# The sign and exponent biases of a top-k attention kernel, made by VectorE in place of ScalarE

## The chip, the cores and the metric

The kernel runs on one core of one Trainium2 chip, as one launch. The metric is the device time of that launch in microseconds, the median of three runs. TensorE (PE), VectorE (DVE), ScalarE (ACT), GpSimd (POOL) and SyncE (SP) work through their own lists in program order, so the order in which the program writes the instructions down is the schedule.

## The reference, cut to what matters

```python
scores = scale * np.matmul(q, k.transpose(0, 1, 3, 2))      # (4, 8, 576, 576), scale = 1/8
kth = np.partition(scores, -32, axis=-1)[..., -32:-31]       # the 32nd largest of each row
scores = np.where(scores >= kth, scores, -1e9)
attn = np.exp(scores - max) ; attn = attn / (sum + 1e-9)     # max, sum over the row
x = (attn @ v), heads side by side: (2304, 512)
h = np.maximum(np.maximum(x @ w1, x @ w2), x @ w3)           # a dense layer, 768 wide
x = h @ w_out
...                                                          # then 8 experts, top 1, 1024 wide
```

## The kernel before, in words

The attention is cut into 144 tiles of 128 query rows by 576 keys, and four tiles make a group `g`, one tile of it having the number `i`. A hand-written loop over a step number `t` issues, at each step, one stage of each of some twelve tiles: the scores of tile t + 2 (PE, L892), the copy of the scores of tile t + 1 out of PSUM into `s` (ACT, L899), the candidate maxima of tile t (DVE, six L921 of 96 columns each, into `c`), and so on back to the product with v of tile t - 14. The dense layer and the first expert slots are fitted in between as units, and from about 700 us on the rest of the experts runs alone (the tail).

The top 32 of a row are found so. On DVE `st_rounds` takes the 48 candidates of a tile through three rounds of eight: L936 writes the eight largest to `T1`, L937 strikes them out, L938 and L939 do the same once more, and L940 writes the third eight to `T3`. The 24th largest candidate (`T3[..., 7]`), with its sign turned and a hair smaller, is the bias `bf`: on ACT, `st_over` takes `Sign(s + bf)` into `g` and counts (L967). On POOL L973 takes `s - g`, and DVE's L982 takes eight maxima of that. From the count and these eight, DVE picks the 32nd value of four tiles at once (L988 to L991, then L1011 and L1012 into `hkth`). L991 also compares with `bf`. Two tiles of a group are then masked on DVE (L1056, `e<-s,hkth,e`), two by way of a second Sign on ACT (L1042) and a subtraction on POOL (L1045). ACT takes the exponential (L1051) with the bias `be`, which is the row's largest value (`T1[..., 0]`) times a constant, for four tiles at once. ACT and POOL then split the result into two float16 halves (L1062, L1066).

What sets the order around the change: `st_rounds` of tile t - 1 is a *chain*, a list of small steps. After each instruction of the `bulk` list (the L921 pairs, the L982, the masks and the subtractions of the splits) `micro` issues one step of each open chain, and `finish` issues what is left of this chain at the end of the step. `st_thr` and `st_over` of tile t - 2 are called straight from the loop, so on ACT `bf` (L957), in every fourth tile also `be` (L946), and the Sign stand behind the L899 of the same step. Where `general` is true, the code belongs to a second attempt, which runs only if the first one missed; it did not run here.

```python
nc.scalar.activation(out=be[g], in_=T1[g][:, :, 0:1], func=ACTF.Copy, scale=-ESC)                          # L946, 128x4
nc.scalar.activation(out=bf[g][:, i], in_=T3[g][:, i, 7:8], func=ACTF.Copy, scale=-(1.0 - 2.0 ** -21))     # L957, 128x1
nc.scalar.activation(out=gg[n], in_=Ss[n], func=ACTF.Sign, bias=bf[g][:, i], accum_out=cnt[g][:, i])       # L967
```

`T1`, `T3`, `bf`, `be`, `cnt`, `s` and `e` lie in SBUF. The tile `vec`, with `y8`, lies in PSUM.

Of the kernel before, what the change touches and what calls it, by code (L numbers as in the profile page):

```python
# [7 lines left out]
F32 = mybir.dt.float32  # L8
# [3 lines left out]
ACTF = mybir.ActivationFunctionType  # L12
ALU = mybir.AluOpType
# [6 lines left out]
def kernel(  # L20
# [14 lines left out]
    nc = tc.nc  # L35
# [5 lines left out]
    P = 128  # L41
# [23 lines left out]
    ESC = 1.0 / (float(D) ** 0.5 * SC * SC * DOWN)  # L65
# [16 lines left out]
    G = 4  # L82
# [12 lines left out]
    def attempt(ctx, general):  # L95
# [531 lines left out]
        with ExitStack() as p1:  # L627
# [3 lines left out]
            sm_p = p1.enter_context(tc.tile_pool(name="sm", bufs=3))  # L631
# [47 lines left out]
            def chain(fns):  # L679
                chains.append(list(fns))  # L680
                return chains[-1]
# [198 lines left out]
            Sps, Ss, T1, T3, zz, bf, be, cnt, y8, kth, ff, ee, pt = ({} for _ in range(13))  # L880
# [43 lines left out]
            def st_rounds(n):  # L924
                g, i = divmod(n, G)
                if i == 0:
                    T1[g] = sm_p.tile([P, G, 8], F32, tag="T1", name="T1", bufs=2)
                    if not general:
                        T3[g] = sm_p.tile([P, G, 8], F32, tag="T3", name="T3", bufs=2)
                if general:  # L930
                    return chain([lambda: nc.vector.max(out=T1[g][:, i], in_=Ss[n])])
                c = cands.pop(n)
                c2 = sm_p.tile([P, CAND * 8], F32, tag="c2", name="c2", bufs=1)
                t2 = sm_p.tile([P, 8], F32, tag="t2", name="t2", bufs=1)
                ops = [
                    lambda: nc.vector.max(out=T1[g][:, i], in_=c),  # L936
                    lambda: nc.vector.match_replace(out=c2, in_to_replace=T1[g][:, i], in_values=c, imm_value=LOW),  # L937
                    lambda: nc.vector.max(out=t2, in_=c2),  # L938
                    lambda: nc.vector.match_replace(out=c, in_to_replace=t2, in_values=c2, imm_value=LOW),  # L939
                    lambda: nc.vector.max(out=T3[g][:, i], in_=c),  # L940
                ]
                return chain(ops)

            def st_bias(g):
                be[g] = sm_p.tile([P, G, 1], F32, tag="be", name="be")
                nc.scalar.activation(out=be[g], in_=T1[g][:, :, 0:1], func=ACTF.Copy, scale=-ESC)  # L946

            def st_thr(n):
                g, i = divmod(n, G)
                if general:  # L950
                    if i == G - 1:
                        st_bias(g)
                    return
                if i == 0:
                    cnt[g] = sm_p.tile([P, G, 1], F32, tag="cnt", name="cnt")
                    bf[g] = sm_p.tile([P, G, 1], F32, tag="bf", name="bf")
                nc.scalar.activation(out=bf[g][:, i], in_=T3[g][:, i, 7:8], func=ACTF.Copy, scale=-(1.0 - 2.0 ** -21))  # L957
                if i == G - 1:
                    st_bias(g)

            def st_over(n):

# [595 lines left out]
            with tc.manual_schedule():  # L1558
# [42 lines left out]
                while second is None or not fin() or len(ranked) < NTT:  # L1601
# [12 lines left out]
                    if ok(t - 1):  # L1614
                        must.append(st_rounds(t - 1))
# [27 lines left out]
                    if ok(n):  # L1643
                        st_thr(n)
                        st_over(n)
# [127 lines left out]
```

## Time and profile before

| | |
|---|---|
| median of 3 runs | 924.04 us (923.32 to 924.06) |
| the profiled execution | 919.08 us, of which 917.4 us lie between its first and last instruction (the span) |
| busy over the span | PE 741.1 us (81%), DVE 745.3 (81%), ACT 705.7 (77%), POOL 597.5 (65%) |
| L957 on ACT | 144 times, from 28.1 to 662.4 us |
| L946 on ACT | 36 times, from 47.0 to 662.4 us |

Busy time is the time in which an engine has at least one instruction of the program in work, waits inside an instruction among it. Neighbouring instructions of DVE and of ACT overlap by some 0.1 us, so what an instruction costs its engine is the distance from its start to the next one's start, and not its duration. In a list of waits the engine on the left was idle, and the instruction on the right of the arrow is what ended it. The chain is the work that ended last, followed back from the last instruction.

### The profile page before, as it was taken

The page shows a single profiled execution, that of the slowest core. Times are in us where ns is not written, and L with a number is a line of the kernel's source. Part 1 is how long each engine was busy: PE and PEld are TensorE (multiplying, and loading weights), DVE is VectorE, ACT ScalarE, POOL GpSimd, SP SyncE. Part 2 cuts the span into 40 slices and gives each one's busy share as a digit, 9 for nine tenths or more (in the row PEclk, how much of TensorE's full clock was granted, in tenths as well). Part 3 has the DMA queues.
Part 4 walks back from the last instruction along what each step waited for, and adds up shares of the span by engine and source line. Part 5 has one row for each costly group of instructions (what it writes and reads, how often), then busy time and mean ns, then how long its engine had stood idle before and what let it go on. Part 6 is the DMA issues. An engine that isn't in the chain of part 4 may idle for free.

```text
span 917.4 us, 29131 instructions
## 1 busy us (share of the span) xinstructions
PE 741.1 (81%) x10606; PEld 573.4 (63%) x10606; DVE 745.3 (81%) x3108; ACT 705.7 (77%) x1464; POOL 597.5 (65%) x554
## 2 busy tenths in 40 slices
PE   1112367888878799978988899989999999999993
PEld 0000236576655678757767688757987756687882
DVE  5999998999999999999998999998852426476661
ACT  4768999999999999999997999998862231566661
POOL 2556788898988699887877889888992220211110
PEclk9999999999998999999989999999999999999997
DMA  9872977767997888799989788988977459699270
GB/s 223 262 232 51 222 148 152 128 135 133 194 167 162 157 153 169 150 201 173 175 167 172 167 158 155 179 173 148 188 153 128 128 170 298 173 298 258 60 223 16
DMA packets 372164, 155.93 MB, mean 170 GB/s; under 512 B 331931, under 2 KB 348319, under 8 KB 372000
## 3 DMA queue, kind: packets, MB, share of 16 engines
q1 hardware_dynamic: 368128, 143.10, 75.0%
q0 software_dynamic: 3136, 9.46, 3.3%
q8 instruction: 87, 1.43, 0.7%
q10 hardware_dynamic: 736, 1.32, 0.4%
q14 instruction: 77, 0.63, 0.2%
HBM read 76.06 MB, written 16.67 MB: 101 GB/s over the span
## 4 chain that ended last, share of the span: by engine, by line
PE 29%; ACT 20%; issue 19%; DVE 17%; POOL 8%; DMA 4%; SPq 1%; POOLq 0%; ACTq 0%; DVEq 0%
PE mm L355 15%; ACT g L967 4%; DVE c L921 4%; PE av L1085 4%; ACT s L899 3%; PE S L892 3%; ACT e L1051 3%; ACT phl L1062 2%; POOL phl L1066 2%; DVE vec L982 2%; POOL f L973 2%; PE mm L1178 2%; DVE e L1056 2%; PE mm L1179 2%; PE mm L1180 2%
## 5 line engine op out<-in xcount | busy, mean ns | idle before, releaser
L355 PEld LDWEIGHTS <-W 128*128 128x128 f16 x4560 | 248.5, 100 | 19.6 <-issue 16.5
L355 PE MATMUL mm<-xT,W 128*128 128x128 f16 x3456 | 214.3, 224 | 13.3 <-DVE vl L746 5.6
L973 POOL TENSOR_TENSOR f<-s,g 128x576 f32<-128x576 f32 x144 | 184.1, 1278 | 40.4 <-ACT g L967 24.2
L1066 POOL TENSOR_TENSOR phl<-e,phl 128x576 f16<-128x576 f32 x144 | 188.2, 1307 | 6.5 <-ACT phl L1062 5.7
L921 DVE MAX8 c<-s 128x8 f32<-128x96 f32 x864 | 175.0, 243 | 9.4 <-ACT s L899 5.6
L892 PEld LDWEIGHTS <-qT 128*128 128x128 f16 (+1 forms) x640 | 56.6, 107 | 189.8 <-issue 155.2
L892 PE MATMUL S<-kt,qT 128*128 128x64 f16 (+3 forms) x320 | 61.9, 345 | 107.2 <-ACT s L899 91.5
L1051 ACT ACTIVATE e<-s,be 128x576 f32<-128x576 f32 x144 | 109.8, 762 | 14.6 <-POOL phl L1066 10.9
L1085 PE MATMUL av<-vh,pt 128*128 128x65 f16 (+3 forms) x1600 | 110.6, 200 | 11.4 <-DVE xn L1134 9.8
L967 ACT ACTIVATE g<-s,bf 128x576 uint16<-128x576 f32 x144 | 111.7, 775 | 5.6
L982 DVE MAX8 vec<-f 128x8 f32<-128x576 f32 x144 | 108.7, 755 | 4.7 <-POOL f L973 1.9
L1045 POOL TENSOR_TENSOR s<-s,g 128x576 f32<-128x576 f32 x72 | 92.6, 1286 | 24.0 <-DVE e L1056 22.3
L1085 PEld LDWEIGHTS <-pt 128*128 128x128 f16 (+3 forms) x2400 | 89.3, 103 | 24.2 <-issue 11.0
L899 ACT ACTIVATE s<-S 128x576 f32<-128x576 f32 x144 | 91.6, 636 | 12.3 <-PE S L892 11.9
L1062 ACT ACTIVATE phl<-e 128x576 f16<-128x576 f32 x144 | 96.2, 668 | 5.9 <-DMA pt<-phl 5.9
L1085 PE MATMUL av<-vl,pt 128*128 128x64 f16 (+3 forms) x800 | 100.1, 197 | 0.0
L461 DVE SCALAR_TENSOR_TENSOR W<-st,W 128x1024 f16<-128x1024 f32 x56 | 65.8, 1220 | 37.3 <-ACT W L460 28.7
L1056 DVE SCALAR_TENSOR_TENSOR e<-s,hkth,e 128x576 f32<-128x576 f32 x72 | 85.4, 1186 | 12.7 <-ACT e L1051 8.0
L892 PE MATMUL S<-kT,qT 128*128 128x512 f16 (+3 forms) x320 | 48.6, 292 | 22.5 <-ACT s L899 22.4
L1169 POOL TENSOR_TENSOR hhl<-a,hhl 128x384 f16<-128x384 f32 x36 | 37.6, 1046 | 33.5 <-ACT hhl L1168 32.3
L460 ACT ACTIVATE W<-st 128x1024 f16<-128x1024 f32 x56 | 55.6, 1046 | 1.8 <-DMA st<-in_moe_w_dram 1.8
L1042 ACT ACTIVATE g<-s,hkth 128x576 uint16<-128x576 f32 x72 | 54.7, 760 | 0.0
(233 smaller groups left out, 1568.6 us busy)
## 6 DMA issues: line engine op xcount, KB each, us to landing
st<-in_moe_w_dram SPq DMA_DIRECT2D x72, 512.0 KB
st<-in_moe_w_dram SPq DMA_DIRECT2D x28, 256.0 KB
raw<-in_moe_w_dram SPq DMA_DIRECT2D x12, 512.0 KB
st<-in_v_dram SPq DMA_DIRECT2D x16, 256.0 KB
hs<-he SPq DMA_DIRECT2D x16, 256.0 KB
hTe<-hs SPq DMA_DIRECT2D x8, 512.0 KB
st<-in_q_dram SPq DMA_DIRECT2D x15, 256.0 KB
qT<-qT SPq DMA_DIRECT2D x30, 128.0 KB
```

The lines of the kernel that those rows point to most:

```text
L355: nc.tensor.matmul(out=ps[:, o * n:(o + 1) * n], lhsT=w(b, kk, c), rhs=x(a, kk), start=(kk == 0 and i == 0), stop=(kk == KD - 1 and i == 2))
L892: nc.tensor.matmul(out=ps[o:o + m, j, 0:(REM if j else NQ * P)], lhsT=qt[:, vv, hh, 0:m], rhs=kr[:, hh] if j else km[:, hh // HG, :, hh % HG],
L899: nc.scalar.activation(out=s, in_=Sps.pop(n).rearrange("p a b -> p (a b)")[:, 0:S], func=ACTF.Copy, scale=DOWN)
L921: nc.vector.max(out=c[:, i * 8:(i + 1) * 8], in_=s[:, i * CW:(i + 1) * CW])
L967: nc.scalar.activation(out=gg[n], in_=Ss[n], func=ACTF.Sign, bias=bf[g][:, i], accum_out=cnt[g][:, i])
L973: let_in(nc.gpsimd.tensor_tensor(out=ff[n], in0=Ss[n], in1=gg.pop(n).bitcast(F16), op=ALU.subtract))
L982: bulk.append(lambda: nc.vector.max(out=y8[g][:, i, 1:9], in_=y))
L1051: nc.scalar.activation(out=e, in_=Ss.pop(n) if early(n) else Ss[n], func=ACTF.Exp, scale=ESC, bias=be[g][:, i])
L1056: masked.append(nc.vector.scalar_tensor_tensor(out=e, in0=Ss.pop(n), scalar=kth[g][:, i:i + 1], in1=e, op0=ALU.is_ge, op1=ALU.mult))
L1062: nc.scalar.activation(out=ph[:, 0, 0:S], in_=p, func=ACTF.Copy)
L1066: nc.gpsimd.tensor_tensor(out=ph[:, 1, 0:S], in0=p, in1=ph[:, 0, 0:S], op=ALU.subtract)
L1085: nc.tensor.matmul(out=av[o:o + m, i, 0:n], lhsT=t[0:kk, p * NCH + c, o:o + m], rhs=v_rows(x, b, c, hh)[:, 0:n], start=(c == 0 and p == 0 ...
```

## The change

DVE makes both biases. `bf` becomes the last step of the chain of `st_rounds`, and in the fourth tile of a group `be` becomes the step before it; in the other tiles that step is empty, so that an instruction of `bulk` can come between L940 and `bf`. `st_thr` no longer does anything in the attempt that runs. From L957 on, line numbers of the changed kernel are lower by one.

```diff
                     lambda: nc.vector.max(out=T3[g][:, i], in_=c),
                 ]
+                if i == 0:
+                    cnt[g] = sm_p.tile([P, G, 1], F32, tag="cnt", name="cnt")
+                    bf[g] = sm_p.tile([P, G, 1], F32, tag="bf", name="bf")
+                ops.append((lambda: st_bias(g)) if i == G - 1 else None)
+                ops.append(lambda: nc.vector.tensor_scalar(out=bf[g][:, i], in0=T3[g][:, i, 7:8], scalar1=-(1.0 - 2.0 ** -21),
+                                                           scalar2=None, op0=ALU.mult))
                 return chain(ops)
 
             def st_bias(g):
                 be[g] = sm_p.tile([P, G, 1], F32, tag="be", name="be")
-                nc.scalar.activation(out=be[g], in_=T1[g][:, :, 0:1], func=ACTF.Copy, scale=-ESC)
+                nc.vector.tensor_scalar(out=be[g], in0=T1[g][:, :, 0:1], scalar1=-ESC, scalar2=None, op0=ALU.mult)
...
-                if i == 0:
-                    cnt[g] = sm_p.tile([P, G, 1], F32, tag="cnt", name="cnt")
-                    bf[g] = sm_p.tile([P, G, 1], F32, tag="bf", name="bf")
-                nc.scalar.activation(out=bf[g][:, i], in_=T3[g][:, i, 7:8], func=ACTF.Copy, scale=-(1.0 - 2.0 ** -21))
-                if i == G - 1:
-                    st_bias(g)
```

ACT's order, at the last two tiles of the tenth group, some 203 to 209 us into the span: before,

```order
L899 ACTIVATE s<-S 128x576
L957 ACTIVATE bf<-T_2707 128x1
L967 ACTIVATE g,cnt<-s,bf 128x576
L1051 ACTIVATE e<-s,be 128x576
L1062 ACTIVATE phl_148<-e 128x576
L1051 ACTIVATE e<-s,be 128x576
L1168 ACTIVATE hhl<-a 128x384
L899 ACTIVATE s<-S 128x576
L957 ACTIVATE bf<-T_2707 128x1
L946 ACTIVATE be<-T_2706 128x4
L967 ACTIVATE g,cnt<-s,bf 128x576
L1042 ACTIVATE g<-s,hkth 128x576
```

and with the change:

```order
L899 ACTIVATE s<-S 128x576
L966 ACTIVATE g,cnt<-s,bf 128x576
L1050 ACTIVATE e<-s,be 128x576
L1061 ACTIVATE phl_148<-e 128x576
L1050 ACTIVATE e<-s,be 128x576
L1167 ACTIVATE hhl<-a 128x384
L899 ACTIVATE s<-S 128x576
L966 ACTIVATE g,cnt<-s,bf 128x576
L1041 ACTIVATE g<-s,hkth 128x576
```

The Sign follows the copy of the scores directly, and the two small instructions are gone; nothing else has moved on ACT.

DVE's order, at the end of the step that makes the thresholds of the last of these tiles (at 204 us): before,

```order
L939 MATCH_REPLACE c<-t_3029,c_3028 128x48
L1163 TENSOR_TENSOR a<-a,mm 128x384
L940 MAX T_2707<-c 128x8
L921 MAX c<-s 128x8 x2
L936 MAX T_3091<-c 128x8
L1219 TENSOR_SCALAR se<-se 128x1
```

and with the change:

```order
L939 MATCH_REPLACE c<-t_3030,c_3029 128x48
L1162 TENSOR_TENSOR a<-a,mm 128x384
L940 MAX T_2710<-c 128x8
L952 TENSOR_SCALAR be<-T_2709 128x4
L946 TENSOR_SCALAR bf<-T_2710 128x1
L921 MAX c<-s 128x8 x2
L936 MAX T_3094<-c 128x8
L1218 TENSOR_SCALAR se<-se 128x1
```

Both biases stand between L940 and the first L921 of the next tile.

DVE's order one step earlier (at 200 us), where the bulk list still holds something when L940 is issued: before,

```order
L988 TENSOR_TENSOR hsel<-vec,cnt 128x36
L940 MAX T_2707<-c 128x8
L746 TENSOR_TENSOR hl<-mm,hl 128x8x64
L1163 TENSOR_TENSOR a<-a,mm 128x384
L990 COPY vec<-T_2342 128x4
L991 SCALAR_TENSOR_TENSOR heq<-vec,bf 128x4
```

and with the change:

```order
L987 TENSOR_TENSOR hsel<-vec,cnt 128x36
L940 MAX T_2710<-c 128x8
L746 TENSOR_TENSOR hl<-mm,hl 128x8x64
L1162 TENSOR_TENSOR a<-a,mm 128x384
L946 TENSOR_SCALAR bf<-T_2710 128x1
L989 COPY vec<-T_2345 128x4
L990 SCALAR_TENSOR_TENSOR heq<-vec,bf 128x4
```

`bf` comes two instructions behind L940 here. Of the 144, 40 stand as at the place above, directly behind L940 or with only `be` between; 10 stand between L990 and L991, 6 between two of L863, L866 and L868, and 88 elsewhere.

## Rows read from the trace of the kernel before

**Rows 1.** The page, part 1: busy us, share of the span, instructions.

```profile
PE 741.1 (81%) x10606; PEld 573.4 (63%) x10606; DVE 745.3 (81%) x3108; ACT 705.7 (77%) x1464; POOL 597.5 (65%) x554
```

**Rows 2.** Stretches: from:to, length, each engine's busy us (x), clock, DMA share, GB/s.

```profile
30.00:100.00 70.00, 15.29 (x78) 7.23 (x78) 68.10 (x241) 54.27 (x118) 41.75 (x37) 1.00 0.66 177
100.00:600.00 500.00, 423.88 (x6370) 338.57 (x6370) 474.94 (x2263) 467.25 (x1029) 430.68 (x372) 0.97 0.85 163
500.00:600.00 100.00, 93.68 (x1566) 78.06 (x1563) 96.35 (x449) 94.63 (x211) 86.09 (x75) 0.98 0.84 166
600.00:665.00 65.00, 61.65 (x906) 49.05 (x904) 56.11 (x270) 57.97 (x130) 57.94 (x51) 0.97 0.93 168
```

**Rows 3.** DVE's waits from 100 to 600 us: us in total, times, longest.

```profile
DVE e L1056 <- ACT e L1051: 5.0, 10, 1.1
DVE hl L746 <- ACT mm L745: 5.0, 5, 2.7
DVE c L921 <- ACT s L899: 2.2, 5, 0.9
DVE W1h L746 <- ACT mm L745: 1.1, 2, 0.8
```

**Rows 4.** The page, part 4: the chain that ended last, by engine.

```profile
PE 29%; ACT 20%; issue 19%; DVE 17%; POOL 8%; DMA 4%; SPq 1%; POOLq 0%; ACTq 0%; DVEq 0%
```

**Rows 5.** ACT's L957 and L946 by shape, 0 to 665 us: busy, mean ns, idle.

```profile
L957 ACT ACTIVATE bf<-T 128x1 f32<-128x1 f32 x144 | 28.0, 194 | 0.0
...
L946 ACT ACTIVATE be<-T 128x4 f32<-128x4 f32 x36 | 7.2, 200 | 0.0
```

**Rows 6.** ACT in order of time, 203 to 208 us: start, us, instruction.

```profile
203.06 0.19 ACT L957 ACTIVATE bf<-T 128x1 f32<-128x1 f32 x1
203.29 0.78 ACT L967 ACTIVATE g<-s,bf 128x576 uint16<-128x576 f32 x1
...
207.19 0.19 ACT L957 ACTIVATE bf<-T 128x1 f32<-128x1 f32 x1
207.28 0.20 ACT L946 ACTIVATE be<-T 128x4 f32<-128x4 f32 x1
207.41 0.77 ACT L967 ACTIVATE g<-s,bf 128x576 uint16<-128x576 f32 x1
```

**Rows 7.** DVE in order of time, 204 to 205 us.

```profile
204.26 0.21 DVE L940 MAX8 T<-c 128x8 f32<-128x48 f32 x1
204.57 0.42 DVE L921 MAX8 c<-s 128x8 f32<-128x96 f32 x2
204.91 0.19 DVE L936 MAX8 T<-c 128x8 f32<-128x48 f32 x1
205.02 0.14 DVE L1219 TENSOR_SCALAR se<-se 128x1 f32<-128x1 f32 x1
205.07 0.17 DVE L1272 TENSOR_TENSOR vec<-mm,base 128x8 f32<-128x8 f32 x1
```

**Rows 8.** POOL in order of time, the same stretch.

```profile
204.25 1.28 POOL L1066 TENSOR_TENSOR phl<-e,phl 128x576 f16<-128x576 f32 x1
```

**Rows 9.** The only 128x144 TENSOR_SCALAR, DVE, in order of time.

```profile
685.49 0.61 DVE L1019 TENSOR_SCALAR hit<-hkth 128x144 f16<-128x144 f32 x1
```

**Rows 10.** POOL in order of time, at the same place.

```profile
684.72 1.28 POOL L1045 TENSOR_TENSOR s<-s,g 128x576 f32<-128x576 f32 x1
```

**Rows 11.** Line L1056: duration ns min/median/max, first and last start, form.

```profile
L1056 DVE SCALAR_TENSOR_TENSOR e<-s,hkth,e x72: 797/1110/3109, 73.8 to 678.8; 128x576 f32<-128x576 f32 x72
```

**Rows 12.** DVE groups over the whole span: count, busy us, mean ns, idle.

```profile
L1056 DVE SCALAR_TENSOR_TENSOR e<-s,hkth,e 128x576 f32<-128x576 f32 x72 | 85.4, 1186 | 12.7 <-ACT e L1051 8.0 <-ACT phl L1062 3.8
...
L1219 DVE TENSOR_SCALAR se<-se 128x1 f32<-128x1 f32 x18 | 2.5, 138 | 0.0
```

**Rows 13.** L957 alone, by stretch: from:to, length, ACT busy (count).

```profile
30.00:100.00 70.00, 2.56 (x12) 1.00 0.66 177
100.00:600.00 500.00, 22.33 (x116) 0.97 0.85 163
```

**Rows 14.** L946 alone, by stretch.

```profile
30.00:100.00 70.00, 0.65 (x3) 1.00 0.66 177
100.00:600.00 500.00, 5.75 (x29) 0.97 0.85 163
```

More of the change, by code (lines that the diff above doesn't have):

```diff
@@ L952, in st_thr @@
                         st_bias(g)
-                    return
-                if i == 0:
-                    cnt[g] = sm_p.tile([P, G, 1], F32, tag="cnt", name="cnt")
-                    bf[g] = sm_p.tile([P, G, 1], F32, tag="bf", name="bf")
-                nc.scalar.activation(out=bf[g][:, i], in_=T3[g][:, i, 7:8], func=ACTF.Copy, scale=-(1.0 - 2.0 ** -21))
-                if i == G - 1:
-                    st_bias(g)
             def st_over(n):
```

## The prediction

> **What bounds the kernel now.** I read the busy shares first. Over the whole span PE and DVE are equal at 81% and ACT follows with 77% [rows 1], which says little, because the work comes in stages. Cut into stretches [rows 2], the attention part shows what matters. From 30 to 100 us DVE is busy for 68.10 of 70 us, 97.3%, while ACT is busy for 54.27, 78%: DVE alone sets the pace, and 97.3% is what it reaches when it does. From 100 to 600 us DVE is busy for 474.94 of 500 us (95%) and ACT for 467.25 (93%). Two engines both stand near their limit, and each now and then waits for the other: the largest waits of DVE there are all for ACT, 5.0 + 5.0 + 2.2 + 1.1 = 13.3 us [rows 3]. From 500 us on PE is as full as they are (93.68 of 100, then 61.65 of 65). The chain says the same from another side: ACT has 20% of the span, DVE 17%, PE 29%, and no engine has most of it [rows 4]. The change takes work from the second fullest engine of this part and gives it to the fullest.
>
> The profiled execution took 919.08 us, 1.7 us more than its span and 5.0 us (0.5%) less than the median of 924.04. I work out a difference against it and add that to the median. A difference under 0.2%, 1.8 us, is about what a measurement of this kernel cannot tell from none.
>
> **What ACT loses.** 144 instructions L957 and 36 L946 [rows 5]. Durations of 194 and 200 ns are not their price, since neighbours overlap. From the start of L957 to that of the Sign is 0.23 us, and with L946 between them 0.22 us [rows 6], so L946 lies inside the time in which the Sign waits for L957's result. The Sign can stand where L957 stood: 144 x 0.23 = 33 us less on ACT. ACT never sat idle ahead of either (the last column of rows 5), so all of it is time of a working engine. No DMA and no queue is moved.
>
> **What DVE gains: bf.** The nearest row is L1219, a TENSOR_SCALAR of 128x1 from SBUF to SBUF. It starts at 205.02 and its successor at 205.07, so it costs 0.05 us [rows 7], and its mean duration over 18 is 138 ns [rows 12]. It does not mind POOL: L1066 was at work from 204.25 to 205.53 [rows 8]. Of the 144 new ones, 88 stand where nothing is waited for: 88 x 0.05 = 4.4 us. The 40 directly behind L940 cost nothing, I take it: there DVE waits already, since L940 ends at 204.47 and L921 starts at 204.57, 0.31 us behind L940's start [rows 7]. With `bf` there, L940's 0.21, a short wait, and 0.14 less the usual overlap of 0.08 make about the same; if `bf` has to wait as long as L921 did, it is 0.06 more each, 2.4 us. The last 16 stand between an instruction and one that uses its result; they cost 0 to 0.05 each, and I take 0. Together 4.4 us, between 4.4 and 7.6.
>
> **What DVE gains: be.** No row before shows a 128x4 from SBUF to SBUF. Two rows bound it. By L1219, one value per row, it would run beside POOL and vanish behind L940 like `bf`: 0 us. By L1019, a TENSOR_SCALAR of 128x144 from SBUF to SBUF, it would not: that one starts at 685.49 and takes 0.61 us [rows 9], while POOL's L1045 is at work until 686.00 [rows 10]. It ends at 686.10, 0.10 us behind POOL's. The masks show the same: L1056 takes 797 ns at the least and up to 3109 [rows 11], 1186 in the mean [rows 12], so POOL holds a mask up for 389 ns on average. I take `be` to be held like these, since L1019 is the only row of its kind with more than one value in a row of the tile: 36 x 0.389 = 14.0 us. The upper end is half of POOL's 1.28 us at the 86% that POOL is busy from 100 to 600 us [rows 2, 8], 0.55 us, or 19.8 us in all.
>
> What the notes make of it: the Trainium skill (page SBUF — State Buffer, section Who interferes with whom) says that a `tensor_scalar` from SBUF to SBUF can run on two ports, of which one pair is shared with GpSimd, and that whichever of the two engines comes later then waits until the other's instruction is through. Its page VectorE: DVE Perf Modes, section What auto-detection actually checks, gives the condition as one source, both ends in SBUF and even (or equal) outermost counts. By that rule four values count among the held ones and the 14.0 stays; by the row of L1219 alone it would be 0. The trace agrees at 128x144 and shows no 128x4.
>
> **The new waits.** The Sign now waits for `bf` on DVE instead of L957 waiting for L940. At the place of rows 6 and 7 L940 ends at 204.47 and L957 reads its result at 207.19, 2.7 us later. `bf` comes at most a few instructions behind L940 (two at the third place of the order, a subtraction and a maximum). So the wait is covered; if DVE falls further behind, the Sign, behind it the exponential and the next copy of scores L899, and with them POOL's L973 and PE's scores wait too, but then DVE sets the pace and they wait for nothing else. Behind a held `be` stand `bf` and the six L921 of the next tile, on DVE itself.
>
> **The sum.** From 100 to 600 us lie 116 of the 144 L957 and 29 of the 36 L946 [rows 13, 14]. DVE gets 116/144 x 4.4 + 29 x 0.389 = 3.5 + 11.3 = 14.8 us more, 489.7 in all. ACT falls to about 440, out of the way, and DVE paces as from 30 to 100 us: 489.7 / 0.973 = 503.3 us, **3.3 us more**. From 30 to 100 us it is 12/144 x 4.4 = 0.4, and 3 x 0.389 scaled by POOL's lower load there (41.75 of 70 us, 60%, against 86%) = 0.8: 1.2 us, paid in full, since DVE paces already. From 600 to 665 us PE is the fuller one (61.65 against DVE's 56.11), and 2 us more on DVE cost nothing. The tail has neither bias and only starts later. 3.3 + 1.2 = 4.5 us: 923.6 us for the profiled execution's like, 928.5 for the median. With the upper ends of both prices (29 x 0.55 + 116/144 x 7.6 = 22.1 from 100 to 600, 1.8 before) it is (474.94 + 22.1) / 0.973 - 500 + 1.8 = 12.6 us, 937.
>
> **Rivals.**
> - *ACT's relief decides, and the time falls.* The mechanism: a `be` of four values is not held. DVE then gets 3.5 us from 100 to 600 us, and its pace allows (474.94 + 3.5) / 0.973 = 491.7, 8.3 us less. The chain gives the same: ACT's 20% are 183 us, 29% of the 635 us from 30 to 665, and 29% of 33 is 9.5 us saved, less DVE's 25% of 4.4, 1.1. But from 500 us on PE is at its limit, so four fifths of 8.3 remain, 6.6, less the 0.4 before 100 us: some 6 us, **918**, at best 916. For it speaks that DVE's waits are for ACT; against it, that L1019 was held. The point from which it decides: a mean hold of `be` under some 0.15 us, where DVE's new work stays under 8 us. The Trainium skill (page Perfetto Trace Analysis, section Optimizing Scalar/DVE Operations) puts ScalarE's overhead at about 93 ns an instruction on SBUF; by it I estimate 180 x 0.093 = 17 us of relief and 921 for this rival. The rows disagree: 0.23 us for each tile.
> - *The two cancel.* `be` is held, but all 13.3 us that DVE waits for ACT go away, and what it gets is 14.8: 1.5 us more, and the 1.2 before 100 us fit into the 1.9 that DVE is not busy there: **925.5**, no change to a measurement. For it: ACT becomes earlier by 0.23 us a tile and DVE later, so few waits should survive. Against it: 5.0 us of them are five waits for L745, one of 2.7 us [rows 3], which 0.23 us a tile does not cover.
>
> **How the numbers follow.** The forecast has 0.47: two rows of different make show the hold, and DVE has no room. Its own range is 925 to 937, and about 0.41 of it is slower by over 0.2%, 0.06 is not. The first rival has 0.31, nearly all of it faster. The second has 0.22: 0.16 the same, 0.04 slower, 0.02 faster. That makes 0.32 faster, 0.23 the same, 0.45 slower. The predicted time is 928.5. The range reaches from just above the first rival's best, 917, to the end of the held case, 937.
>
> **What would show it.** Right: the new 128x4 group has a mean well over 0.3 us and instructions that end with POOL's; the new 128x1 group has some 0.14. DVE is busy for about 490 of the 500 us from 100 to 600, its waits for ACT shrink from 13 us to a few, and ACT is busy for some 25 us less and waits for DVE more. Wrong: a 128x4 of 0.15 us throughout; DVE's share at or under 95%; or a Sign that waits for `bf` for microseconds, in which case the forecast has the wrong engine.

## The result and the profile after

| | before | changed |
|---|---|---|
| median of 6 runs | 924.05 us (923.32 to 926.06) | 932.99 us (930.01 to 936.23) |
| ratio | | 1.0094, interval 1.0071 to 1.0118 |
| the profiled execution (its span) | 919.08 us (917.4) | 931.81 us (930.1) |

The change costs 8.9 us by the medians, about 1%, where 4.5 were forecast. The two profiled executions differ by 12.7 us, because the one of before was 5.0 us under its median and this one is 1.2 under. I read *where* the time went from the profiles, and *how much* from the ratios.

The page of the changed kernel, part 1 and the first line of the chain, against [rows 1, 4]:

```profile
PE 744.7 (80%) x10606; PEld 578.5 (62%) x10606; DVE 774.8 (83%) x3288; ACT 680.4 (73%) x1284; POOL 595.6 (64%) x554
...
DVE 47%; PE 19%; issue 17%; DMA 5%; ACT 4%; POOL 4%; SPq 2%; POOLq 0%; DVEq 0%; ACTq 0%
```

ACT is 25.3 us less busy and has all but left the chain (20% to 4%). DVE is 29.5 us busier and now has nearly half of it (17% to 47%). Where those 29.5 us lie is told by DVE's groups by shape, over the whole span (count | busy us, mean ns | idle before):

```profile
L1055 DVE SCALAR_TENSOR_TENSOR e<-s,hkth,e 128x576 f32<-128x576 f32 x72 | 71.9, 998 | 5.6 <-ACT phl L1061 3.1 <-ACT e L1050 2.4
...
L952 DVE TENSOR_SCALAR be<-T 128x4 f32<-128x4 f32 x36 | 44.8, 1243 | 0.0
...
L946 DVE TENSOR_SCALAR bf<-T 128x1 f32<-128x1 f32 x144 | 21.9, 152 | 0.5
```

A `be` writes four values a row and takes 1.24 us in the mean; a `bf` writes one and takes 0.15. The masks, L1056 of before [rows 12], are quicker than they were, 998 ns against 1186. The line's durations (ns, min/median/max) say that the mean of `be` is made by a few:

```profile
L952 DVE TENSOR_SCALAR be<-T x36: 140/554/7027, 42.1 to 669.7; 128x4 f32<-128x4 f32 x36
L946 DVE TENSOR_SCALAR bf<-T x144: 131/144/1274, 24.9 to 675.3; 128x1 f32<-128x1 f32 x144
```

0.14 us is what a 128x4 takes when nothing holds it; 7.03 us is the longest. Six of the 36 last 2.9 us or more. DVE in order of time (start, us, instruction), first an ordinary case and then the six:

```profile
189.05 0.56 DVE L952 TENSOR_SCALAR be<-T 128x4 f32<-128x4 f32 x1
189.52 0.14 DVE L946 TENSOR_SCALAR bf<-T 128x1 f32<-128x1 f32 x1
...
219.79 4.81 DVE L952 TENSOR_SCALAR be<-T 128x4 f32<-128x4 f32 x1
224.51 0.14 DVE L946 TENSOR_SCALAR bf<-T 128x1 f32<-128x1 f32 x1
...
257.49 2.94 DVE L952 TENSOR_SCALAR be<-T 128x4 f32<-128x4 f32 x1
...
332.88 4.78 DVE L952 TENSOR_SCALAR be<-T 128x4 f32<-128x4 f32 x1
...
527.61 7.03 DVE L952 TENSOR_SCALAR be<-T 128x4 f32<-128x4 f32 x1
...
583.19 3.58 DVE L952 TENSOR_SCALAR be<-T 128x4 f32<-128x4 f32 x1
...
669.73 5.63 DVE L952 TENSOR_SCALAR be<-T 128x4 f32<-128x4 f32 x1
```

And POOL in order of time at the first two of these places:

```profile
188.30 1.28 POOL L972 TENSOR_TENSOR f<-s,g 128x576 f32<-128x576 f32 x1
189.54 1.27 POOL L1065 TENSOR_TENSOR phl<-e,phl 128x576 f16<-128x576 f32 x1
...
219.59 1.27 POOL L972 TENSOR_TENSOR f<-s,g 128x576 f32<-128x576 f32 x1
220.82 1.27 POOL L1065 TENSOR_TENSOR phl<-e,phl 128x576 f16<-128x576 f32 x1
222.06 1.27 POOL L972 TENSOR_TENSOR f<-s,g 128x576 f32<-128x576 f32 x1
223.30 1.27 POOL L1065 TENSOR_TENSOR phl<-e,phl 128x576 f16<-128x576 f32 x1
```

At 189 us POOL's subtraction ends at 189.58, `be` ends at 189.61, and POOL's next instruction, started at 189.54, runs beside `bf`. That is the hold that was forecast: the rest of one instruction of POOL. At 219.79 it goes another way. `be` starts while POOL is in one instruction (to 220.86), is not let through at its end, nor at the end of the second and the third, and ends at 224.60, 0.03 us behind the *fourth* (224.57), when POOL had nothing more to start. All six end so: POOL is then idle for 1.9 to 3.3 us, until DVE lets its next instruction go on. Behind a held `be` DVE stands still, and so does everything that DVE feeds. The six cases make 28.8 of the 44.8 us. The other 30 make 16.0, and are held for 0.39 us each above the unheld 0.14.

From 100 to 600 us (columns as in [rows 2]):

```profile
100.00:600.00 500.00, 417.15 (x6166) 333.55 (x6166) 485.05 (x2346) 436.92 (x862) 418.44 (x364) 0.95 0.84 159
```

DVE is at 97.0% of the stretch, the pace that it kept before 100 us in [rows 2], and ACT at 87%. The granted clock of PE is 0.95 there against 0.97; that this is no cause is seen below in e1, which has 0.95 too and loses nothing.

The delay arises in the attention part and stays. The line of L940 (one per tile; first and last start; below it who waited for it, us and times), before and after:

```profile
L940 DVE MAX8 T<-c x144: 187/200/213, 23.7 to 658.5; 128x8 f32<-128x48 f32 x144
...
  POOL f L973: 5.3, 7
```

```profile
L940 DVE MAX8 T<-c x144: 188/202/214, 23.6 to 669.6; 128x8 f32<-128x48 f32 x144
...
  POOL f L972: 21.2, 12
```

The first tile is level and the last 11.1 us late. POOL, which passed `be` by, then has to wait itself: its subtraction waits for DVE's next L940 for 21.2 us in all, against 5.3, and 15.8 of them are the five waits behind the first five long holds. On the way, L940 of tiles 47, 63, 79, 95, 111 and 127 (counted from 0) comes 2.9, 6.4, 9.4, 9.1, 7.7 and 14.1 us later than before: the delay steps up across the long holds at 220, 257, 333, 528 and 583 us and does not grow between 383 and 527 us, where there is none.

### The profile page after: what moved, and what is told of

Same layout as the page of the kernel before. It is cut to its first block, busy times and chain, and to the rows that moved or that the text cites. A ratio compares the mean times of both kernels' runs of the same rounds, so it can differ in the third digit from the quotient of the medians.

```text
span 930.1 us, 29063 instructions
## 1 busy us (share of the span) xinstructions
PE 744.7 (80%) x10606; PEld 578.5 (62%) x10606; DVE 774.8 (83%) x3288; ACT 680.4 (73%) x1284; POOL 595.6 (64%) x554
## 4 chain that ended last, share of the span: by engine, by line
DVE 47%; PE 19%; issue 17%; DMA 5%; ACT 4%; POOL 4%; SPq 2%; POOLq 0%; DVEq 0%; ACTq 0%
DVE c L921 10%; PE mm L355 10%; DVE vec L981 7%; DVE e L1055 4%; DVE be L952 4%; PE av L1084 2%; DVE c L939 2%; DVE c L937 2%; DVE a L1162 2%; DVE hl L746 2%; PE S L892 1%; DVE T L940 1%; POOL out_dram L405 1%; DVE T L936 1%; DVE t L938 1%
## 5 line engine op out<-in xcount | busy, mean ns | idle before, releaser
L355 PEld LDWEIGHTS <-W 128*128 128x128 f16 x4560 | 252.7, 101 | 23.8 <-issue 20.9
L355 PE MATMUL mm<-xT,W 128*128 128x128 f16 x3456 | 216.7, 225 | 15.9 <-DVE vl L746 5.8
L972 POOL TENSOR_TENSOR f<-s,g 128x576 f32<-128x576 f32 x144 | 185.1, 1285 | 50.1 <-DVE T L940 21.2
L921 DVE MAX8 c<-s 128x8 f32<-128x96 f32 x864 | 174.8, 245 | 3.6 <-ACT s L899 3.5
L1044 POOL TENSOR_TENSOR s<-s,g 128x576 f32<-128x576 f32 x72 | 92.6, 1286 | 30.8 <-DVE e L1055 27.3
L899 ACT ACTIVATE s<-S 128x576 f32<-128x576 f32 x144 | 92.5, 643 | 23.8 <-PE S L892 21.9
L1055 DVE SCALAR_TENSOR_TENSOR e<-s,hkth,e 128x576 f32<-128x576 f32 x72 | 71.9, 998 | 5.6 <-ACT phl L1061 3.1
L1168 POOL TENSOR_TENSOR hhl<-a,hhl 128x384 f16<-128x384 f32 x36 | 34.9, 970 | 32.0 <-ACT hhl L1167 29.3
```

The lines of the kernel that those rows point to most:

```text
L355: nc.tensor.matmul(out=ps[:, o * n:(o + 1) * n], lhsT=w(b, kk, c), rhs=x(a, kk), start=(kk == 0 and i == 0), stop=(kk == KD - 1 and i == 2))
L921: nc.vector.max(out=c[:, i * 8:(i + 1) * 8], in_=s[:, i * CW:(i + 1) * CW])
L972: let_in(nc.gpsimd.tensor_tensor(out=ff[n], in0=Ss[n], in1=gg.pop(n).bitcast(F16), op=ALU.subtract))
L1044: let_in(nc.gpsimd.tensor_tensor(out=Ss[n], in0=Ss[n], in1=zz.pop(n).bitcast(F16), op=ALU.subtract))
L1055: masked.append(nc.vector.scalar_tensor_tensor(out=e, in0=Ss.pop(n), scalar=kth[g][:, i:i + 1], in1=e, op0=ALU.is_ge, op1=ALU.mult))
```

## The experiments

My theory was that `be` on DVE is held by POOL's instructions and that this makes the kernel slower. The rivals: that DVE is too full for any new work, and that the wait of the Sign for `bf` does it. Each kernel is compared with the kernel before on the same chip, whose median was 923.59 us for e1 to e4, 919.49 for e6, e8 and e9, and 921.42 for e10.

**e1: `bf` on DVE, `be` back on ACT.** The changed kernel with

```diff
-                ops.append((lambda: st_bias(g)) if i == G - 1 else None)
+                ops.append(None)
...
-                nc.vector.tensor_scalar(out=be[g], in0=T1[g][:, :, 0:1], scalar1=-ESC, scalar2=None, op0=ALU.mult)
+                nc.scalar.activation(out=be[g], in_=T1[g][:, :, 0:1], func=ACTF.Copy, scale=-ESC)
```

and `st_thr` calling `st_bias` in the fourth tile, as before.

> Only the 128x1 bias bf stays on VectorE; the 128x4 be is back on ScalarE, ahead of the Sign in every fourth tile. Theory H (the loss is the hold of be behind GpSimd, 44.8 us of VectorE in the changed kernel): VectorE gets some 4 us, ScalarE loses 144 x 0.23 less 36 x 0.1 = 29 us, and the time falls below that of before, to 914 to 922 us; the masks L1055 go back to a mean of about 1.2 us. Theory S (VectorE is full, so that every small instruction on it costs, and the Sign waits for bf): bf is still there, and the time stays at 930 us or more.

Measured: 921.37 us, ratio 0.998 (0.9957 to 1.0004). The whole loss is gone. The masks are held again. Groups of e1 by shape:

```profile
L1054 DVE SCALAR_TENSOR_TENSOR e<-s,hkth,e 128x576 f32<-128x576 f32 x72 | 81.8, 1136 | 11.5 <-ACT e L1049 11.1
...
L946 DVE TENSOR_SCALAR bf<-T 128x1 f32<-128x1 f32 x144 | 20.9, 145 | 1.4
```

and its stretch from 100 to 600 us:

```profile
100.00:600.00 500.00, 422.60 (x6357) 339.40 (x6357) 477.06 (x2374) 448.41 (x912) 429.89 (x371) 0.95 0.87 163
```

ACT is 18.8 us less busy there than before, and the kernel is hardly faster. What became of this is read from ACT's waits in the stretch (us in total, times, longest), before and in e1:

```profile
ACT e L1051 <- POOL phl L1066: 10.0, 13, 1.2
ACT s L899 <- PE S L892: 6.7, 9, 1.8
...
ACT e L1051 <- POOL s L1045: 1.4, 3, 0.8
```

```profile
ACT e L1049 <- POOL phl L1064: 14.5, 17, 1.2
ACT s L899 <- PE S L892: 12.3, 13, 2.6
ACT e L1049 <- POOL s L1043: 6.3, 10, 1.3
```

The same three waits grow from 18.1 to 33.1 us: most of what ACT was relieved of it now spends waiting for POOL's split, for PE's scores and for POOL's subtraction.

**e2: `be` alone on DVE, `bf` left on ACT.** The kernel before with

```diff
+                ops.append((lambda: st_bias(g)) if i == G - 1 else None)
...
-                nc.scalar.activation(out=be[g], in_=T1[g][:, :, 0:1], func=ACTF.Copy, scale=-ESC)
+                nc.vector.tensor_scalar(out=be[g], in0=T1[g][:, :, 0:1], scalar1=-ESC, scalar2=None, op0=ALU.mult)
...
-                if i == G - 1:
-                    st_bias(g)
```

> Only be moves to VectorE; bf is made by ScalarE as before. Theory H: the hold is there without most of ScalarE's relief, since be alone lies in the shadow of bf on ScalarE: 932 to 942 us, with a mean of be well over 0.5 us. Theory S: 36 instructions more on VectorE are nothing, 923 to 926 us.

Measured: 937.01 us, ratio 1.0153 (1.0099 to 1.0207), with holds as in the changed kernel:

```profile
L947 DVE TENSOR_SCALAR be<-T x36: 140/643/7028, 41.5 to 674.6; 128x4 f32<-128x4 f32 x36
```

36 instructions, with no Sign waiting for `bf` on DVE, cost as much as the whole change, and by the ratios more (the intervals overlap). So the loss does not need `bf` or its new wait.

**e3: the same values on DVE, one per row at a time.** The changed kernel with

```diff
-                ops.append((lambda: st_bias(g)) if i == G - 1 else None)
+                if i == 0:
+                    be[g] = sm_p.tile([P, G, 1], F32, tag="be", name="be")
+                ops.append(lambda: nc.vector.tensor_scalar(out=be[g][:, i], in0=T1[g][:, i, 0:1], scalar1=-ESC,
+                                                           scalar2=None, op0=ALU.mult))
```

> Both biases on VectorE, but be by tile: four instructions of 128x1 in place of one of 128x4, each ahead of the bf of its tile. Theory H: none of them is held (0.14 us each, 0.05 us of VectorE's time), 108 more instructions cost 5 us of VectorE at most, and the time is 915 to 923 us, under that of before. Theory S: more small instructions, 934 us or more.

Measured: 923.36 us, ratio 0.9996 (0.9969 to 1.0023): level with before, and not under it as expected.

```profile
L947 DVE TENSOR_SCALAR be<-T x144: 123/137/153, 24.6 to 659.1; 128x1 f32<-128x1 f32 x144
```

DVE does the same multiplications in four times as many instructions, 288 new ones in all, and not one of the 144 was held, though 36 of them stand where the 128x4 stood. So it is the shape of `be`, not DVE's load, that costs.

**e4: POOL's next subtraction waits for `be`.** The changed kernel with

```diff
-                nc.vector.tensor_scalar(out=be[g], in0=T1[g][:, :, 0:1], scalar1=-ESC, scalar2=None, op0=ALU.mult)
+                ins = nc.vector.tensor_scalar(out=be[g], in0=T1[g][:, :, 0:1], scalar1=-ESC, scalar2=None, op0=ALU.mult)
+                if not general:
+                    masked.append(ins)
```

so that POOL's next subtraction of the lines L972 and L1044, as the program issues them, is let in only when `be` is through. The kernel before does this for the masks already: `masked` is the list of what such a subtraction has to wait for.

> The changed kernel, in which GpSimd's next subtraction s - g waits for be, as it waits for a mask already. Theory H with the port lost several times in a row (be held through up to six GpSimd instructions, up to 7.0 us): a hold now ends with at most one or two GpSimd instructions, no be is over 2.6 us, the sum falls from 44.8 to 15 to 22 us, and the time to 925 to 930 us. Theory S: 932 to 934 us, as without the wait; if GpSimd's new wait costs more than the hold, above 934.

Measured: 926.5 us, ratio 1.0018 (0.9993 to 1.0043). The time came out as expected; the holds did not shrink as far:

```profile
L952 DVE TENSOR_SCALAR be<-T 128x4 f32<-128x4 f32 x36 | 28.4, 790 | 0.0
...
525.32 4.33 DVE L952 TENSOR_SCALAR be<-T 128x4 f32<-128x4 f32 x1
```

The sum is 28.4 us and not 15 to 22, the longest 4.33 and not at most 2.6. POOL's order of time at the longest shows why:

```profile
526.24 1.27 POOL L974 TENSOR_TENSOR f<-s,g 128x576 f32<-128x576 f32 x1
527.48 1.26 POOL L1067 TENSOR_TENSOR phl<-e,phl 128x576 f16<-128x576 f32 x1
528.71 0.90 POOL L1170 TENSOR_TENSOR hhl<-a,hhl 128x384 f16<-128x384 f32 x1
529.82 1.28 POOL L974 TENSOR_TENSOR f<-s,g 128x576 f32<-128x576 f32 x1 [0.20 <-DVE bf L946]
```

The gate stood in front of one subtraction further back, and the instructions already queued ahead of it still passed `be` one after another, until POOL ran out at 529.61 and `be` ended at 529.65. A shorter run of POOL's still went with shorter holds and less time; the gate was badly placed.

**e6: `be` as 128x3 and 128x1.** The changed kernel with

```diff
-                nc.vector.tensor_scalar(out=be[g], in0=T1[g][:, :, 0:1], scalar1=-ESC, scalar2=None, op0=ALU.mult)
...
+                for c in (slice(0, G - 1), slice(G - 1, G)):
+                    nc.vector.tensor_scalar(out=be[g][:, c], in0=T1[g][:, c, 0:1], scalar1=-ESC, scalar2=None, op0=ALU.mult)
```

> The changed kernel, with be made by two instructions: 128x3 and 128x1. Which shapes are held? Theory any-width (all with more than one value for each partition are held): the 128x3 is held like the 128x4 was, mean over 0.5 us and a sum near 45 us, and the time is 930 to 936 us. Theory even-only (only an even count can be halved among two ports): no instruction of either shape is over 0.2 us, and the time is 919 to 924 us, as with be made tile by tile.

Measured: 928.73 us, ratio 1.0095 (1.0073 to 1.0117), the same loss as the change (the expected times were on a scale of 924).

```profile
L956 DVE TENSOR_SCALAR be<-T 128x3 f32<-128x3 f32 x36 | 41.1, 1141 | 0.0
```

An odd count is held like four. What is free is the single value per row; two values were not tried. The 128x1 behind it has 0.14 us in the median, and 0.41 and 1.34 us in two places, where it started behind a held 128x3 and ended with it.

**e8 and e9: e1 and the changed kernel again,** unaltered, on the chip of e6, to set the two against each other.

> The kernel with bf on VectorE and be on ScalarE once more, for its interval: 0.998 [0.9957, 1.0004] at first. Theory that ScalarE's relief is worth a little: a ratio of 0.996 to 0.999 with an interval under 1. Theory that it is worth nothing, since VectorE, GpSimd and PE pace: 0.999 to 1.001.

> The changed kernel unaltered, on the chip of the two runs beside it: 931 to 935 us, ratio 1.007 to 1.012, a sum of the holds of be of 40 to 50 us, some of them through three or more GpSimd instructions. If the long holds were an accident of one profile, their sum would be nearer to 14 us, and some of the loss would have another cause.

Measured: e8 917.86 us, ratio 0.9984 (0.997 to 0.9999); e9 928.0 us, 1.0103 (1.0073 to 1.0133), the ratio as expected. So `be` on DVE alone makes 10.1 us by the medians, 11.0 by the ratios, between two kernels that differ in nothing else. e8 is the only version whose interval lies below 1, and its gain, 0.16%, is under what I called measurable. e9's `be` sums to 45.1 us, and its long ones stand at 219.44, 257.09, 331.09, 526.40, 581.37 and 667.47 us with 4.78, 2.93, 4.76, 6.48, 3.57 and 5.61 us: the same six places in a second profile. So they are no accident of one execution. They seem to hang on the schedule: e2, with `bf` left on ACT, has the one at 220 us and the longest as well, but at 381.59 us one of 3.97 that is not among the six.

**e10: the price of `bf` by itself.** The kernel before, ACT unchanged, with DVE computing `bf` a second time, at the changed kernel's place, into a tile `bd` that nothing reads:

```diff
+            bd = {}
...
+                if i == 0:
+                    bd[g] = sm_p.tile([P, G, 1], F32, tag="bd", name="bd")
+                ops.append(None)
+                ops.append(lambda: nc.vector.tensor_scalar(out=bd[g][:, i], in0=T3[g][:, i, 7:8], scalar1=-(1.0 - 2.0 ** -21),
+                                                           scalar2=None, op0=ALU.mult))
```

> The kernel before, with bf made a second time on VectorE into a tile that nobody reads; ScalarE keeps both biases and all its work. It prices VectorE's 144 small instructions alone. Theory C (they cost what the sum gave them, 88 x 0.05 us, and what ScalarE loses is worth some us): ratio 1.002 to 1.006, 925.5 to 929.5 us on a scale of 924. Theory N (they vanish in gaps, and ScalarE's relief of 29 us is worth only the 1 to 2 us that the kernel with bf on VectorE and be on ScalarE gained): ratio 0.999 to 1.001.

Measured: 925.19 us, ratio 1.0049 (1.0029 to 1.0068).

```profile
L946 DVE TENSOR_SCALAR bd<-T 128x1 f32<-128x1 f32 x144 | 21.0, 146 | 1.4
```

144 instructions of 0.146 us, with 1.4 us of idle time ahead of them in all, cost 0.49%, some 4.5 us. The interval allows 2.7 to 6.3.

## Why the prediction was right, and which term was off

On a scale of 924 us the ratios take the change apart, each step measured by two kernels that differ in it. The steps add up to e9 by construction; what they can be held against is the change as first measured, in the last line:

| step | from | us |
|---|---|---|
| DVE makes `bf` as well | e10 against before | +4.5 |
| ACT is relieved of `bf` | e8 (0.9984) against e10 (1.0049) | -6.0 |
| `be` on DVE in place of ACT | e9 (1.0103) against e8 | +11.0 |
| sum, e9 | | +9.5 |
| the change as first measured | 1.0094 | +8.7 |

The second step compares ratios from two chips, and the intervals add to some 3 us there.

The mechanism of the forecast, `be` held by POOL and DVE paying for it, is what the runs show. The size of its main term was wrong by nearly three times, and that the time lies within the range all the same is in part luck, as the bullets on `be` and on the masks show.

- **What ACT loses: right.** 33 us were worked out. In the median the Sign started 0.125 us behind the end of L899 before, and starts 0.104 us ahead of it now: 0.23 us a tile, as worked out. ACT is busy for 30.3 us less from 100 to 600 us (467.25 to 436.92; "about 440" was forecast), in part because fewer tiles fall into the stretch now. Over the whole span it is 25.3, since the time in which the Sign waited for L957's result was no busy time. Its chain share falls by 16 points.
- **What ACT's relief is worth: the direction right.** It gives 6 us, and DVE's `bf` takes 4.5 of them back; e1's waits show the rest given up to POOL and PE. The first rival's condition, an unheld `be`, was met in e1, e3 and e8, and its result, 6 us net, was not: they give 1.9, 0.4 and 1.5. Had it decided, the time would have been some 922 to 924 and not 918.
- **`bf`: right.** 4.4 us were priced, 4.5 measured. 0.05 us, from one start to the next beside L1219 [rows 7], was about the right price (in e10 it is 0.06 where nothing is waited for), and 0.14 us, the duration, would have been 20 us. The 40 behind L940 cost nothing, as taken: in e1 the first L921 starts 0.31 us behind L940's start, as before (medians of 307 and 304 ns). That the sum agrees to 0.1 us is closer than e10's interval can tell. 143 of 144 were not held. The one of 1.27 us started behind a held `be` and ended with it at 141.61 us, as did the maxima behind it, so these lines tell of no hold of its own:

```profile
140.22 1.39 DVE L952 TENSOR_SCALAR be<-T 128x4 f32<-128x4 f32 x1
140.34 1.27 DVE L946 TENSOR_SCALAR bf<-T 128x1 f32<-128x1 f32 x1
140.41 1.20 DVE L921 MAX8 c<-s 128x8 f32<-128x96 f32 x2
140.74 0.88 DVE L936 MAX8 T<-c 128x8 f32<-128x48 f32 x1
```
- **`be` held like L1019 and the masks: right in kind, and here the size failed.** "36 x 0.389 = 14.0 us" took the masks' mean hold [rows 11, 12] for that of `be`, with one instruction of POOL's as the most that could be waited for ("half of POOL's 1.28 us", 19.8 us in all). It measured 1243 ns, 1.1 us above the unheld 0.14, 39.8 us over 36, twice the upper end. For 30 of the 36 the price was right, 0.39 us each; the other six make the difference. The bound was wrong because `be` can lose at the end of POOL's instruction as well, and again. The row that could have told it was in front of me: a mask of 3109 ns [rows 11] against a shortest of 797 was held for 2.3 us, more than one instruction of POOL's. DVE and POOL of the kernel before, in order of time, at this mask:

```profile
523.18 3.11 DVE L1056 SCALAR_TENSOR_TENSOR e<-s,hkth,e 128x576 f32<-128x576 f32 x1 [0.83 <-ACT e L1051]
```

```profile
523.18 1.26 POOL L973 TENSOR_TENSOR f<-s,g 128x576 f32<-128x576 f32 x1
524.41 1.26 POOL L1066 TENSOR_TENSOR phl<-e,phl 128x576 f16<-128x576 f32 x1
526.43 1.28 POOL L973 TENSOR_TENSOR f<-s,g 128x576 f32<-128x576 f32 x1 [0.76 <-DVE T L940]
```

The mask starts with L973, loses to L1066 at 524.41 as well, and gets through when that ends at 525.67. A mean hides this. Nor were the masks a like case: POOL's next subtraction has to wait for a mask (e4), and none is made to wait for `be`. How much shorter that makes the masks' holds no run shows.
- **What kept the miss small: an exchange with the masks.** Their busy time fell by 13.5 us (85.4 to 71.9). Before, the four longest masks start at 223, 329, 523 and 662 us (2.25, 2.24, 3.11 and 2.38 us); in the changed kernel none of 2 us or more is left there, and four of the long `be` start at 220, 333, 528 and 670 us. In e1, with `be` gone from DVE, masks of the same lengths are back at 221, 328, 523 and 664 us. So these look like stretches in which POOL has a long queue, and whichever instruction of the held kind comes into them first pays: now it is `be`, a little earlier, with more of POOL's queue ahead of it. The forecast knew nothing of this exchange; it was luck. DVE got 29.5 us more busy time over the span where 18.4 (4.4 and 14.0) were forecast.
- **DVE's pace: right.** It is 97.0% of 100 to 600 us (485.05; "about 490 of the 500" did not fit the forecast's own 97.3%), where 97.3% was taken [rows 2]. The 1.2 us before 100 us were not kept: tile 15, at 111 us, is 1.2 late and tile 31, at 174 us, is level again. Put into the forecast's own formula, 116 of 144 parts of the 29.5 give (474.94 + 23.8) / 0.973 - 500 = 12.6 us, an estimate; tile 127, whose L940 starts at 603.2 us, is 14.1 late in the trace. The two profiled executions lie further apart than the medians, as said above.
- **The new wait of the Sign: as forecast, covered.** It adds up to 4.3 us in six waits from 100 to 600 us, of 1.2 at the longest; in e1, where `be` is off DVE, it is one wait of 0.5. A wait of 1.9 us, near what the prediction called a sign of the wrong engine, stands at 675.45 us, right behind the hold at 669.73. Like that one, the longest of the six stands right behind a hold, the one at 219.79, which makes it. ACT in order of time:

```profile
224.68 0.78 ACT L966 ACTIVATE g<-s,bf 128x576 uint16<-128x576 f32 x1 [1.24 <-DVE bf L946]
```

- **DVE's waits for ACT: right in direction.** The four of [rows 3] were 13.3 us; in the changed kernel the same four are 7.3 us from 100 to 600 us, more than the "few" that were forecast.

```profile
DVE hl L746 <- ACT mm L745: 3.5, 3, 1.8
DVE c L921 <- ACT s L899: 1.8, 4, 0.6
DVE e L1055 <- ACT e L1050: 1.1, 2, 0.7
...
DVE W1h L746 <- ACT mm L745: 0.9, 2, 0.5
```

- **The second rival** needed the waits to vanish and `be` to cost no more than 14 us; neither came about.
- **The rule of the port.** The Trainium skill (page SBUF — State Buffer, section Who interferes with whom) lets the engine that comes later wait until the other is through. The trace agrees that an SBUF-to-SBUF `tensor_scalar` of four values waits (0.56 us at 189.05). Waiting "until the other is through" is not what 219.79 shows, where three further instructions of POOL's began after `be` and went first; there the measurement decides. The prediction took the rule at its word. By the Trainium skill (page VectorE: DVE Perf Modes, section What auto-detection actually checks), even *or equal* counts qualify, and e6's 128x3 agrees at 1141 ns.

**Left open:** what decides who goes at a hand-over. Where `be` lost in the six long holds, POOL's next instruction starts 32 to 36 ns before the end of its last one (37 and 48 beside one short one); where `be` won, mostly 38 to 51 ns before, but four times 32 to 34 (189.58, 383.14, 510.15 and 637.91 us). In the long holds POOL's queue was ready all along; that does not suffice, since it was ready at 189.58 too.

## What to carry to other kernels

A small SBUF-to-SBUF `tensor_scalar` with more than one value per row is not small beside a busy GpSimd: price it by the longest run of instructions that GpSimd can have queued there, not by the rest of one, or write it one value per row at a time (e3: 144 of these cost less than 36 of those). A source in PSUM may be another way, which no run tried: L1132 of the kernel before, a 128x4 `tensor_scalar` that reads PSUM, takes 131 to 154 ns in all of its 36 places. Read the maximum of a line's durations, and not its mean, to see whether a hold can outlast one instruction. And where three engines stand within a few per cent of each other, some 29 us off one (ACT without `bf`, the estimate ahead of e1) were worth 6, and e1's waits show where most of it went.

## What was not expected of the hardware

A VectorE instruction was held through six GpSimd instructions in a row, one already at work and five that began behind it and went first (from 527.53 to 534.61 us, with `be` ending at 534.64): 7.03 us for one that takes 0.14 alone. The long holds stand at the same six places of the schedule in both profiles of the changed kernel, and the longest in e2 as well (7.028 us). Three values per row are held like four, 1141 against 1243 ns, while e3's single ones ran in 123 to 153 ns beside the same GpSimd work.
